# The last block's output projection by seven half products, two tile pairs in turn, with its stores in halves on two queues

## Chip, cores, metric

The kernel runs on one core of one Trainium2 chip. The metric is the device time of one execution in microseconds (us). Most executions agree within 0.3%, so a difference of a few tenths of a microsecond in one profile needs care.

## The reference, cut to what matters

```python
def reference(q, k, v, moe_w_gate, moe_w_val, moe_w_out):
    attn = attention(q, k, v)          # 8 batches x 8 heads x 576 positions x 64, causal window of 128 ... cut
    x = attn.transpose(0, 2, 1, 3).reshape(4608, 512)
    g = x @ moe_w_gate                 # 512 -> 1536
    return (g * sigmoid(g) * (x @ moe_w_val)) @ moe_w_out      # 1536 -> 512, float32 out
```

The kernel takes the 4608 tokens in nine blocks of 512. Block n (0 to 7) holds positions 0 to 511 of batch n, which are 512 neighbouring rows of the output. Block 8 is the last and holds the remaining 64 positions of each of the eight batches, so a tile of 128 of its tokens is two pieces of 64 rows, far apart in the output.

## The kernel before

A block has gate and value products (`wide`, on TensorE), an activation (ScalarE), two elementwise operations (VectorE) that give `hT`, and the projection of `hT` with `wo`. Blocks 1 to 7 project by Strassen's scheme: the 512 tokens by 512 columns are a 2 x 2 of blocks, and seven products stand in for eight. It runs on two pairs of token tiles, t = 0 and 1, each giving tile t (`top`) and tile t + 2 (`low`). The sums of `hT` that it needs are made on VectorE.

```python
def rows_of(n, j):
    if n == 8:
        return [(0, 64, 2 * j * S + 512), (64, 128, (2 * j + 1) * S + 512)]
    return [(0, 128, n * S + j * P)]

def last_project(n, j):                                  # tile 3 of the last block; tiles 0 to 2 by project()
    osb = opool.tile([P, DM], FP32, name="osb", tag="osb")
    for half in range(2):
        c = slice(half * DM // 2, (half + 1) * DM // 2)
        po = ps_a.tile([P, DM // 2], FP32, name="po", tag="a", bufs=4)
        for m in range(NMB):                             # 12 matmuls of 256 columns
            nc.tensor.matmul(po, hT[n][:, m, j * P:(j + 1) * P], wo_sb[:, m, c], ...)
        # half 0: nc.scalar.mul, half 1: nc.vector.tensor_scalar_mul, into osb[:, c]; then one store per piece of rows,
        # the first on nc.sync, the second on nc.scalar

def strassen(n, t):                                      # blocks 1 to 7
    # ... cut: views of hT and of its sums S2, S3, S4; tiles p1s, p5s, u2s, top, low
    X, Y = po[:, 0, :], po[:, 1, :]                      # the two halves of one PSUM bank
    product(X, A11, B11, True);  nc.scalar.mul(p1s, X, 0.5);  yield      # product = 6 matmuls of 256 columns
    product(p2, A12, B21, True); half_plus(top[:, 0:HC], p2, p1s);  yield
    product(X, S2, T2);          nc.scalar.mul(u2s, X, 0.5);  yield
    product(Y, S1, T1);          nc.scalar.mul(p5s, Y, 0.5);  yield
    product(X, S3, T3);          half_plus(low[:, HC:DM], X, p5s);  yield
    product(Y, S4, B22);         half_plus(top[:, HC:DM], Y, u2s);  yield
    product(X, A22, T4);         nc.scalar.mul(low[:, 0:HC], X, 0.5)
    # ... stores of top and low on nc.sync
```

The softmax here doesn't subtract the row's maximum and nothing guards it: scores larger than these inputs give would overflow.

Of the kernel before, what the change touches and what calls it, by code (L numbers as in the profile page):

```python
# [10 lines left out]
FP32 = mybir.dt.float32  # L11
# [5 lines left out]
P = 128  # L17
# [30 lines left out]
def kernel(  # L48
# [10 lines left out]
    nc = tc.nc  # L59
    B, H, S, D = q.shape  # L60
    NTOK, DM = out.shape
    DFF = moe_w_gate.shape[1]
    NKB = DM // P
    NMB = DFF // P
    NSUP = B // 2
    NBLK = NTOK // 512
# [50 lines left out]
    wo_sb = consts.tile([P, NMB, DM], FP16, name="wo_sb")  # L117
# [9 lines left out]
    supool = ctx.enter_context(tc.tile_pool(name="sup", bufs=4))  # L127
    opool = ctx.enter_context(tc.tile_pool(name="op", bufs=8))
    ps_f = ctx.enter_context(tc.tile_pool(name="ps_f", bufs=3, space=PSUM))
    ps_a = ctx.enter_context(tc.tile_pool(name="ps_a", bufs=4, space=PSUM))  # L130
# [225 lines left out]
    hT = {}  # L356
# [36 lines left out]
    def gate_val(n, m):  # L393
        c0 = 384 if (n, m) in acted else 0
        gate(n, m, wide(n, m, "g"), c0)
        yield
        val(n, m, wide(n, m, "v"), c0)
        yield

    def rows_of(n, j):  # L400
        if n == 8:
            return [(0, 64, 2 * j * S + 512), (64, 128, (2 * j + 1) * S + 512)]
        return [(0, 128, n * S + j * P)]

    def project(n, j, pool, tag, bufs):
        po = pool.tile([P, DM], FP32, name="po", tag=tag, bufs=bufs)
        for m0 in range(0, NMB, 4):
            for i in range(m0, m0 + 4):
                m = NMB - 1 - i if n == 0 else i
                nc.tensor.matmul(po, hT[n][:, m, j * P:(j + 1) * P], wo_sb[:, m, :],  # L410
                                 start=(i == 0), stop=(i == NMB - 1))
            if m0 + 4 == NMB:
                osb = opool.tile([P, DM], FP32, name="osb", tag="osb")
                nc.scalar.mul(osb, po, 0.5)
                for p0, p1, r0 in rows_of(n, j):
                    nc.sync.dma_start(out[r0:r0 + p1 - p0, :], osb[p0:p1, :])
            yield

    def last_project(n, j):

        osb = opool.tile([P, DM], FP32, name="osb", tag="osb")
        for half in range(2):
            c = slice(half * DM // 2, (half + 1) * DM // 2)
            po = ps_a.tile([P, DM // 2], FP32, name="po", tag="a", bufs=4)
            for m in range(NMB):
                nc.tensor.matmul(po, hT[n][:, m, j * P:(j + 1) * P], wo_sb[:, m, c],
                                 start=(m == 0), stop=(m == NMB - 1))
            if half == 0:
                nc.scalar.mul(osb[:, c], po, 0.5)
            else:  # L430
                nc.vector.tensor_scalar_mul(osb[:, c], po, 0.5)
            for i, (p0, p1, r0) in enumerate(rows_of(n, j)):
                (nc.sync if i == 0 else nc.scalar).dma_start(out[r0:r0 + p1 - p0, c], osb[p0:p1, c])
            yield 1.5



# [2 lines left out]
    HC = DM // 2  # L440
# [4 lines left out]
    def weight_sums(c):  # L445

        if c == 0:
            one_more.append(supool.tile([P, 1], FP32, name="one", tag="pin", bufs=1))
            nc.vector.memset(one_more[0], 1.0)
        k = slice(2 * c, 2 * c + 2)  # L450
        for t_, a, b in ((T1, B12, B11), (T3, B22, B12)):
            nc.vector.scalar_tensor_tensor(out=t_[:, k, :], in0=a[:, k, :], scalar=one_more[0],
                                           in1=b[:, k, :], op0=ALU.mult, op1=ALU.subtract)
        nc.vector.tensor_sub(T2[:, k, :], B22[:, k, :], T1[:, k, :])
        nc.vector.tensor_sub(T4[:, k, :], B21[:, k, :], T2[:, k, :])
# [4 lines left out]
    def sums(n, c):  # L460

        if n not in hsum:
            hsum[n] = [spool.tile([P, HM, 256], FP16, name=f"S{i}", tag=f"S{i}") for i in (2, 3, 4)]
        lo, hi = slice(2 * c, 2 * c + 2), slice(HM + 2 * c, HM + 2 * c + 2)
        a11, a12 = hT[n][:, lo, 0:256], hT[n][:, hi, 0:256]
        a21, a22 = hT[n][:, lo, 256:512], hT[n][:, hi, 256:512]
        s2, s3, s4 = (t_[:, lo, :] for t_ in hsum[n])
        nc.vector.tensor_sub(s3, a11, a21)
        nc.vector.tensor_add(a21, a21, a22)
        nc.vector.tensor_sub(s2, a21, a11)  # L470
        nc.vector.tensor_sub(s4, a12, s2)

    def strassen(n, t):

        h = hT[n]
        A11, A12 = h[:, 0:HM, 0:256], h[:, HM:NMB, 0:256]
        S1, A22 = h[:, 0:HM, 256:512], h[:, HM:NMB, 256:512]
        S2, S3, S4 = hsum[n]
        cols = slice(t * P, (t + 1) * P)
        po = ps_f.tile([P, 2, HC], FP32, name="po", tag="po", bufs=1)  # L480
        p2 = ps_a.tile([P, HC], FP32, name="p2", tag="a")
        top, low = (opool.tile([P, DM], FP32, name="osb", tag="osb") for _ in range(2))
        p1s = supool.tile([P, HC], FP32, name="p1s", tag="p1s", bufs=1)
        p5s = supool.tile([P, HC], FP32, name="p5s", tag="p5s", bufs=1)
        u2s = supool.tile([P, HC], FP32, name="u2s", tag="u2s", bufs=1)

        def product(dst, a, b, start=False):
            for m in range(HM):
                nc.tensor.matmul(dst, a[:, m, cols], b[:, m, :], start=(start and m == 0),  # L489
                                 stop=(m == HM - 1), skip_group_check=True)  # L490

        def half_plus(dst, a, b):
            nc.vector.scalar_tensor_tensor(out=dst, in0=a, scalar=0.5, in1=b,
                                           op0=ALU.mult, op1=ALU.add)

        X, Y = po[:, 0, :], po[:, 1, :]
        product(X, A11, B11, True)
        nc.scalar.mul(p1s, X, 0.5)
        yield
        product(p2, A12, B21, True)  # L500
        half_plus(top[:, 0:HC], p2, p1s)
        yield
        product(X, S2, T2)
        nc.scalar.mul(u2s, X, 0.5)
        yield
        product(Y, S1, T1)
        nc.scalar.mul(p5s, Y, 0.5)  # L507
        yield
        product(X, S3, T3)
        half_plus(low[:, HC:DM], X, p5s)  # L510
        yield
        product(Y, S4, B22)
        half_plus(top[:, HC:DM], Y, u2s)
        yield
        product(X, A22, T4)
        nc.scalar.mul(low[:, 0:HC], X, 0.5)
        for j, osb in ((t, top), (t + 2, low)):
            for p0, p1, r0 in rows_of(n, j):
                nc.sync.dma_start(out[r0:r0 + p1 - p0, :], osb[p0:p1, :])
        yield  # L520



    AT = {2, 3, *range(5, 10), *range(11, 18)}
# [1 line left out]
    def ffn():  # L526

        for n in range(NBLK):
            if n > 1:
                parts = chain(strassen(n - 1, 0), strassen(n - 1, 1))  # L530
            if n == 1:
                for j in range(PRE):
                    for _ in project(0, j, ps_f, "po", 1):
                        yield 1.0
            for m in range(NMB):
                for half, _ in enumerate(gate_val(n, m)):
                    yield 1.0
                    if n > 1 and 2 * m + half in AT:
                        next(parts)
                        yield 0.75  # L540
                if n == 1:
                    if m % 2 and PRE + m // 2 < 4:
                        for _ in project(0, PRE + m // 2, ps_f, "po", 1):
                            yield 1.0
                    if m in (2, 4, 6):
                        weight_sums(m // 2 - 1)
                if 0 < n < NBLK - 1 and m >= 9:
                    sums(n, m - 9)
            if n > 1:
                assert next(parts, None) is None  # L550
        for j in range(3):
            for _ in project(NBLK - 1, j, ps_a, "a", 4):
                yield 1.0
        yield from last_project(NBLK - 1, 3)


    loaded = done_t = 0
# [187 lines left out]
```

## Time and profile before

| | before |
|---|---|
| time, median (range) | 356.23 us (356.14 to 356.53), 3 runs |
| last gate or value product ends | 340.15 |
| last matmul ends | 350.56 |
| last store is issued (evacuation ended 351.00) | 351.03 |
| last packet of the last store | 352.88 |
| span ends | 354.46 |

The ends of the last value product, of the last matmul and of the last evacuation are read from the chain of waits; issue and packet times are the trace's instruction and packet records. Three views of the kernel before follow. First, of the page: busy time by engine, and the transfers that bring instructions (packets, MB, share).

```profile
span 354.5 us, 7261 instructions
...
PE 341.5 (96%) x2765; PEld 197.5 (56%) x2765; DVE 273.4 (77%) x599; ACT 178.9 (50%) x355; POOL 106.9 (30%) x132
...
q8 instruction: 21, 0.34, 0.4%
```

The q8 line counts 21 blocks of 16 KB of instructions. Second, the DMA view of the last stores, from 349.4 to 353.4 us, in fortieths of 0.1 us (GB/s):

```profile
GB/s 0 0 0 225 246 184 246 123 205 185 205 246 205 184 266 62 195 205 184 215 369 175 10 0 0 0 0 72 195 184 174 328 215 113 31 0 0 0 0 0
```

From 351.7 to 352.1 nothing moves: the last store has the DMA engines to itself. Third, the issues of the last two stores, each in two halves (duration in ns: shortest, median, longest; then when):

```profile
L433 ACTq DMA_DIRECT2D out_dram<-osb x2: 498/540/583, 349.7 to 351.0; - x2
...
L433 SPq DMA_DIRECT2D out_dram<-osb x2: 467/506/544, 349.8 to 351.0; - x2
```

An issue of 64 rows holds its queue for about half a microsecond.

### The profile page before, as it was taken

The page shows a single profiled execution, that of the slowest core. Times are in us where ns is not written, and L with a number is a line of the kernel's source. Part 1 is how long each engine was busy: PE and PEld are TensorE (multiplying, and loading weights), DVE is VectorE, ACT ScalarE, POOL GpSimd, SP SyncE. Part 2 cuts the span into 40 slices and gives each one's busy share as a digit, 9 for nine tenths or more (in the row PEclk, how much of TensorE's full clock was granted, in tenths as well). Part 3 has the DMA queues.
Part 4 walks back from the last instruction along what each step waited for, and adds up shares of the span by engine and source line. Part 5 has one row for each costly group of instructions (what it writes and reads, how often), then busy time and mean ns, then how long its engine had stood idle before and what let it go on. Part 6 is the DMA issues. An engine that isn't in the chain of part 4 may idle for free.

```text
span 354.5 us, 7261 instructions
## 1 busy us (share of the span) xinstructions
PE 341.5 (96%) x2765; PEld 197.5 (56%) x2765; DVE 273.4 (77%) x599; ACT 178.9 (50%) x355; POOL 106.9 (30%) x132
## 2 busy tenths in 40 slices
PE   7889999999999999999999999999999999999995
PEld 4684555444456655565456555664665566556643
DVE  4867976997987799678986998799878965975540
ACT  6845584555555455665556455455444323332321
POOL 8966655544848445544300100000000000000000
PEclk9999999999999999999999999999999999999999
DMA  9999999999999999999995513311022101101114
GB/s 152 170 186 187 141 176 155 99 147 137 157 142 196 146 158 163 157 167 153 165 62 105 83 39 32 88 33 58 17 75 61 44 2 59 62 0 62 41 42 96
DMA packets 157763, 37.34 MB, mean 105 GB/s; under 512 B 147232, under 2 KB 153248, under 8 KB 157728
## 3 DMA queue, kind: packets, MB, share of 16 engines
q0 software_dynamic: 116224, 18.62, 79.8%
q1 hardware_dynamic: 41056, 17.97, 27.6%
q8 instruction: 21, 0.34, 0.4%
q10 hardware_dynamic: 448, 0.30, 0.3%
q14 instruction: 14, 0.11, 0.1%
HBM read 37.91 MB, written 9.44 MB: 134 GB/s over the span
## 4 chain that ended last, share of the span: by engine, by line
PE 73%; DVE 16%; ACT 7%; issue 3%; DVEq 0%; ACTq 0%
PE pv L369 20%; PE pg L369 20%; PE po L489 14%; PE av L320 4%; DVE uu L384 4%; DVE hT L391 3%; PE ps L255 3%; PE po L410 3%; DVE ex L264 3%; PE p L489 2%; ACT ex L260 2%; PE px L346 2%; ACT tt L383 2%; ACT exc L287 2%; DVE x L323 1%
## 5 line engine op out<-in xcount | busy, mean ns | idle before, releaser
L369 PE MATMUL pg<-xT,wg_sb 128*128 128x512 f16 (+2 forms) x464 | 116.0, 365 | 0.6 <-DVE uu L384 0.3
L369 PE MATMUL pv<-xT,wv_sb 128*128 128x512 f16 (+2 forms) x464 | 114.5, 364 | 0.8 <-DVE uu L384 0.4
L383 ACT ACTIVATE tt<-pg 128x512 f16<-128x512 f32 (+2 forms) x110 | 65.5, 596 | 85.2 <-PE pg L369 81.8
L384 DVE SCALAR_TENSOR_TENSOR uu<-tt,pg 128x512 f16<-128x512 f16 (+2 forms) x109 | 73.4, 674 | 34.6 <-ACT tt L383 33.9
L391 DVE TENSOR_TENSOR hT<-uu,pv 128x512 f16<-128x512 f16 (+2 forms) x110 | 74.0, 673 | 7.1 <-PE pv L369 2.2
L369 PEld LDWEIGHTS <-wv_sb 128*128 128x128 f16 x464 | 42.8, 98 | 37.4 <-issue 3.3
L369 PEld LDWEIGHTS <-wg_sb 128*128 128x128 f16 x464 | 42.5, 98 | 36.1 <-issue 3.5
L260 ACT ACTIVATE ex<-ps 128x512 f16<-128x512 f32 x96 | 50.2, 605 | 10.1 <-PE ps L255 10.1
L169 POOL DMA_DIRECT2D va<-in_v_dram x40 | 34.1, 856 | 53.0 <-PE av L320 36.9
L175 POOL DMA_DIRECT2D qn<-in_q_dram x39 | 33.6, 864 | 24.4 <-DMA qT<-qn 14.8
L175 POOL DMA_DIRECT2D kn<-in_k_dram x39 | 33.2, 859 | 25.7 <-DMA kT<-kn 18.4
L264 DVE TENSOR_TENSOR ex<-ex,m_reg 128x1024 f16<-128x1024 f16 x48 | 32.6, 687 | 10.3 <-ACT ex L260 10.3
L489 PEld LDWEIGHTS <-hT 128*128 128x128 f16 x336 | 31.8, 98 | 15.5 <-issue 3.6
L489 PEld LDWEIGHTS <-S 128*128 128x128 f16 x252 | 23.9, 98 | 11.8 <-issue 2.9
L323 DVE TENSOR_TENSOR x<-av,rec 128x256 f16<-128x256 f32 x72 | 29.0, 420 | 0.6
L489 PE MATMUL po<-T,hT 128*128 128x256 f16 x168 | 23.1, 272 | 0.5
L489 PE MATMUL po<-T,S 128*128 128x256 f16 x168 | 23.0, 273 | 0.6 <-ACT p5s L507 0.6
L287 ACT ACTIVATE exc<-psc 128x512 f16<-128x512 f32 x40 | 21.4, 608 | 3.4 <-PE psc L283 3.4
L347 ACT COPY xT<-px 128x512 f16<-128x512 f16 x24 | 14.1, 586 | 14.9 <-PE px L346 14.8
L320 PEld LDWEIGHTS <-ex 128*128 128x128 f16 x384 | 18.4, 97 | 4.9 <-issue 0.7
L320 PE MATMUL av<-va,ex 128*128 128x65 f16 x384 | 20.4, 193 | 0.5
L410 PE MATMUL po<-wo_sb,hT 128*128 128x512 f16 x84 | 19.7, 379 | 0.0
(74 smaller groups left out, 291.0 us busy)
## 6 DMA issues: line engine op xcount, KB each, us to landing
out_dram<-osb SPq DMA_DIRECT2D x32, 256.0 KB, 2.8
va<-in_v_dram POOLq DMA_DIRECT2D x32, 128.0 KB, 7.5
qn<-in_q_dram POOLq DMA_DIRECT2D x31, 128.0 KB, 8.2
kn<-in_k_dram POOLq DMA_DIRECT2D x31, 128.0 KB, 8.1
wo_sb<-in_moe_w_out_dram POOLq DMA_DIRECT2D x2, 768.0 KB, 9.3
wg_sb<-in_moe_w_gate_dram POOLq DMA_DIRECT2D x2, 512.0 KB, 10.5
wv_sb<-in_moe_w_val_dram POOLq DMA_DIRECT2D x2, 512.0 KB, 11.8
out_dram<-osb SPq DMA_DIRECT2D x6, 128.0 KB, 2.4
```

The source lines that it names most:

```text
L169: nc.gpsimd.dma_start(va[rank][p0:p1, :, 0:D], src)
L175: nc.gpsimd.dma_start(t_[p0:p1], src)
L260: nc.scalar.activation(e[:, o:o + 2, :], banks[q4][par], AF.Exp, scale=scale)
L264: nc.vector.tensor_mul(e[:, o, :], e[:, o, :], reg[:, o, :])
L320: nc.tensor.matmul(av[:, j, :], w, val, start=(n == 0), stop=(n == len(todo) - 1))
L323: nc.vector.tensor_mul(x[:, 4 * half:4 * half + 4, :], av[:, :, 0:D], rec.broadcast_to([P, 4, D]))
L369: nc.tensor.matmul(ps[:, c0:c1], w[:, kb, ms], xT[n][:, kb, c0:c1], start=(kb == 0 and c0 == 0), stop=(kb == NKB - 1 and c1 == 512), skip_ ...
L383: nc.scalar.activation(tt, pg[:, c0:c1], AF.Tanh, scale=0.5)
L384: nc.vector.scalar_tensor_tensor(out=uu, in0=tt, scalar=one if (n, m) == PIN else 1.0, in1=pg[:, c0:c1], op0=ALU.add, op1=ALU.mult)
L391: nc.vector.tensor_mul(hT[n][:, m, c0:c1], acted[(n, m)][1][:, c0:c1], pv[:, c0:c1])
L410: nc.tensor.matmul(po, hT[n][:, m, j * P:(j + 1) * P], wo_sb[:, m, :], start=(i == 0), stop=(i == NMB - 1))
L489: nc.tensor.matmul(dst, a[:, m, cols], b[:, m, :], start=(start and m == 0), stop=(m == HM - 1), skip_group_check=True)
```

## The change

The last block, too, is projected by seven products. As no other products stand between them there, the two pairs take turns. One pair gets other buffers, the evacuations of the seventh products are on VectorE (in the earlier blocks they are on ScalarE), and all of the last block's stores go out on two queues, as only its last tile's did before: the lower 64 rows on sync and the upper 64 on ScalarE's.

```diff
+    def store(n, j, osb, c0=0, c1=512, two=False):
+        for i, (p0, p1, r0) in enumerate(rows_of(n, j)):
+            (nc.scalar if two and i else nc.sync).dma_start(out[r0:r0 + p1 - p0, c0:c1],
+                                                            osb[p0:p1, c0:c1])
-    def last_project(n, j):
...
+        end = n == NBLK - 1
+        pool, tag, bufs = (ps_a, "a", 4) if end and t else (ps_f, "po", 1)
...
         product(X, S3, T3)
         half_plus(low[:, HC:DM], X, p5s)
+        if end and t:
+            store(n, t + 2, low, HC, DM, True)
         yield
         product(Y, S4, B22)
         half_plus(top[:, HC:DM], Y, u2s)
+        store(n, t, top, 0, DM, end)
         yield
         product(X, A22, T4)
-        nc.scalar.mul(low[:, 0:HC], X, 0.5)
...
+        if end:
+            nc.vector.tensor_scalar_mul(low[:, 0:HC], X, 0.5)
+        else:
+            nc.scalar.mul(low[:, 0:HC], X, 0.5)
+        store(n, t + 2, low, 0, HC if end and t else DM, end)
         yield
...
-                if 0 < n < NBLK - 1 and m >= 9:
+                if n > 0 and m >= 9:
                     sums(n, m - 9)
...
-        for j in range(3):
-            for _ in project(NBLK - 1, j, ps_a, "a", 4):
-                yield 1.0
-        yield from last_project(NBLK - 1, 3)
+        ends = [strassen(NBLK - 1, t) for t in range(2)]
+        for t in 7 * (0, 1):
+            next(ends[t])
+            yield 0.75
```

More of the change, by code (lines that the diff above doesn't have):

```diff
@@ L414, in project @@
                 nc.scalar.mul(osb, po, 0.5)
-                for p0, p1, r0 in rows_of(n, j):
-                    nc.sync.dma_start(out[r0:r0 + p1 - p0, :], osb[p0:p1, :])
+                store(n, j, osb)
             yield
-    def last_project(n, j):
-        osb = opool.tile([P, DM], FP32, name="osb", tag="osb")
-        for half in range(2):
-            c = slice(half * DM // 2, (half + 1) * DM // 2)
-            po = ps_a.tile([P, DM // 2], FP32, name="po", tag="a", bufs=4)
-            for m in range(NMB):
-                nc.tensor.matmul(po, hT[n][:, m, j * P:(j + 1) * P], wo_sb[:, m, c],
-                                 start=(m == 0), stop=(m == NMB - 1))
-            if half == 0:
-                nc.scalar.mul(osb[:, c], po, 0.5)
-            else:
-                nc.vector.tensor_scalar_mul(osb[:, c], po, 0.5)
-            for i, (p0, p1, r0) in enumerate(rows_of(n, j)):
-                (nc.sync if i == 0 else nc.scalar).dma_start(out[r0:r0 + p1 - p0, c], osb[p0:p1, c])
-            yield 1.5
     HM = NMB // 2
@@ L479, in strassen @@
         cols = slice(t * P, (t + 1) * P)
-        po = ps_f.tile([P, 2, HC], FP32, name="po", tag="po", bufs=1)
+        end = n == NBLK - 1
+        pool, tag, bufs = (ps_a, "a", 4) if end and t else (ps_f, "po", 1)
+        po = pool.tile([P, 2, HC], FP32, name="po", tag=tag, bufs=bufs)
         p2 = ps_a.tile([P, HC], FP32, name="p2", tag="a")
         top, low = (opool.tile([P, DM], FP32, name="osb", tag="osb") for _ in range(2))
-        p1s = supool.tile([P, HC], FP32, name="p1s", tag="p1s", bufs=1)
-        p5s = supool.tile([P, HC], FP32, name="p5s", tag="p5s", bufs=1)
-        u2s = supool.tile([P, HC], FP32, name="u2s", tag="u2s", bufs=1)
+        if end and t:
+            spare = [opool.tile([P, DM], FP32, name="osb", tag="osb") for _ in range(2)]
+            p1s, p5s, u2s = spare[0][:, 0:HC], spare[0][:, HC:DM], spare[1][:, 0:HC]
+        else:
+            p1s, p5s, u2s = (supool.tile([P, HC], FP32, name=i, tag=i, bufs=1)
+                             for i in ("p1s", "p5s", "u2s"))
         def product(dst, a, b, start=False):
@@ L510, in strassen @@
         half_plus(low[:, HC:DM], X, p5s)
+        if end and t:
+            store(n, t + 2, low, HC, DM, True)
         yield
@@ L513, in strassen @@
         half_plus(top[:, HC:DM], Y, u2s)
+        store(n, t, top, 0, DM, end)
         yield
         product(X, A22, T4)
-        nc.scalar.mul(low[:, 0:HC], X, 0.5)
-        for j, osb in ((t, top), (t + 2, low)):
-            for p0, p1, r0 in rows_of(n, j):
-                nc.sync.dma_start(out[r0:r0 + p1 - p0, :], osb[p0:p1, :])
+        if end:
+            nc.vector.tensor_scalar_mul(low[:, 0:HC], X, 0.5)
+        else:
+            nc.scalar.mul(low[:, 0:HC], X, 0.5)
+        store(n, t + 2, low, 0, HC if end and t else DM, end)
         yield
```

## The prediction

> **What bounds the kernel now.** I read the page's slices first, to see which engine fills the span and where.
>
> ```profile
> PE   7889999999999999999999999999999999999995
> DVE  4867976997987799678986998799878965975540
> ACT  6845584555555455665556455455444323332321
> PEclk9999999999999999999999999999999999999999
> ```
>
> TensorE is at 90% or more in all but the first three slices and the last one, at the full clock (the view of the cores gives 1.000). So the time is TensorE's stream plus what stands before and after it. The change touches the last block only, so next I read the chain that ended last, from 336 us on (columns: start, length, what).
>
> ```profile
> 339.29 0.86 PE pv L369 x4
> 340.15 7.77 PE po L410 x36
> 347.92 2.63 PE po L426 x24
> 350.56 0.02 issue
> 350.58 0.42 DVE osb L431
> ```
>
> The gate and value products of the last block end at 340.15. The last projection is 36 matmuls of 512 columns (0.216 us each) and 24 of 256 columns (0.110 us each), one after the other without a gap: 10.40 us. From 350.56 the tail has nothing of TensorE: 0.44 us until the last evacuation ends at 351.00, then the stores, and the span ends at 354.46, that is **3.90 us** after the last matmul. The whole last projection is on the path; the earlier blocks already use seven products, but the last does not.
>
> **What the Trainium skill says.** "TensorE: Matmul & The Clock Gate", section Back-to-back issue gap, gives 262 cycles of 2.4 GHz for 256 columns and 518 for 512, which is 109 and 216 ns. The trace agrees (2.63/24 and 7.77/36), so a product costs by its columns, and halves are not dearer than wholes. "PSUM — Partial Sum Buffer", section PSUM bank collisions raise a hardware error, asks for a guard by bank, not by address. In the trace the products of a pair, whose two results X and Y share a bank, have waited for the evacuation of the other half:
>
> ```profile
> its engine sat idle before it (us, times) until:
>   issue: 6.5, 19
>   ACT p5s L507: 0.6, 2
> ```
>
> "DMA: Bandwidth & Descriptors", section Issuing engines are not separate DMA queues, says that a second queue saves issue time only, because all run on the same 16 engines; its section Rules for kernel authors adds that two transfers to disjoint partition halves serialize. The trace agrees only in part, see below.
>
> **The change part by part.**
>
> *Products.* Removed: 4 row tiles x 12 products of 512 columns, 10.40 us. Added: 2 pairs x 7 products x 6 matmuls of 256 columns = 84 x 0.1096 = 9.20 us. Saved on the path: **1.20 us**. (Of eight half products one falls away; 1/8 of 10.40 is 1.30, and the 2.5 ns or so that each of more, shorter matmuls carries takes the rest.)
>
> *Sums.* Twelve VectorE operations are added, four for each of three column groups, 0.418 us each by their rows (L468 to L471): 5.0 us on an engine that is idle most of the last 20 us. What they do to TensorE I take from block 7, where the same sums stand at the same place, and compare with block 8 (columns: start, length):
>
> ```profile
> 301.90 0.82 PE L489 MATMUL po<-wo_sb,S 128*128 128x256 f16 x6
> ...
> 308.71 1.02 PE L369 MATMUL pv<-xT,wv_sb 128*128 128x512 f16 x4
> ```
> ```profile
> 332.41 0.82 PE L489 MATMUL po<-wo_sb,S 128*128 128x256 f16 x6
> ...
> 339.13 1.03 PE L369 MATMUL pv<-xT,wv_sb 128*128 128x512 f16 x4
> ```
>
> From the pair's sixth product to the last value product block 7 takes 6.81 us and block 8, without sums, 6.72. So the sums cost 0.09 us there, and E, the end of the last value product, moves from 340.15 to 340.24.
>
> *Are the inputs there in time?* In block 7 the last hT was done 2.60 us after that product's start (311.31 less 308.71), hence at E + 1.58. The first product of each pair needs only early columns (E to E + 1.32); the second needs the last hT at its sixth matmul, at E + 1.86. That fits with 0.28 us to spare. S2 needs two more sums, in series 0.46 + 0.42, or one evacuation more: E + 2.5 to 2.9; its last third is read at E + 3.1. It fits.
>
> *Waits between products of one pair.* An evacuation starts 0.10 us after its product and takes 0.38 (ScalarE) or 0.42 (VectorE); with about 0.05 for the signal the bank is free again 0.53 or 0.57 us after. The other pair's product lies between and lasts 0.66. Hidden, with only 0.09 us to spare; this is what taking the pairs in turn buys.
>
> *The last evacuation* was on VectorE before (0.425) and is so after: nothing. On ScalarE it would be 0.384 but stand behind DMA issues of about half a microsecond there.
>
> TensorE's end: 350.56 + 0.09 - 1.20 = **349.45**.
>
> *Stores.* Here part of it is given back. Before, the outputs left in turn: 256 KB every 2.6 us, with only 128 KB in two queues at the end. After, both pairs finish together. Writing T for the end of the last matmul, the evacuations end and the stores are issued near T - 2.1 (128 KB), T - 1.45 (256), T - 0.8 (256), T - 0.1 (256), T + 0.45 (128): 1 MB in 2.6 us. The last block's stores are cut in halves of 64 rows. What such a store moves is in the DMA view of two stretches, of one store of 128 rows and of two of 64 rows on one queue (GB/s by fortieths):
>
> ```profile
> GB/s 0 0 66 262 393 393 360 426 393 393 295 492 393 230 99 0 0 0 0 0 0 0 0 229 328 295 393 393 492 295 393 393 360 393 197 33 0 0 0 0
> ```
> ```profile
> GB/s 0 0 287 164 205 287 205 164 123 328 123 164 369 41 123 246 287 205 287 164 205 246 164 205 123 287 82 123 42 0 0 0 0 0 0 0 0 0 0 0
> ```
>
> With 128 rows some 390, with 64 rows some 190 GB/s. Against the page, halves on two queues need not be slow together: in the present last store (packets 352.15 to 352.88) the packets of 1 KB take 80 ns while one queue is active and 46 ns while both are. I estimate 320 GB/s with both queues, 0.41 us for 128 KB and 0.82 for 256. A store issued now moves its first packet 1.12 us later (351.03 to 352.15). Then the stores end near T - 0.2, T + 0.75, T + 1.6, T + 2.4 and the last at T + 2.8, where before it was at T + 2.32 (352.88). So the last store, which had the engines to itself, queues for about **0.45 us**.
>
> Sum: -1.20 + 0.09 + 0.45 = -0.66; 356.23 becomes **355.6 us**.
>
> **The rivals.**
> *The stores hide.* If the transfers overlap fully, the tail is 3.90 us as before, and the time 355.1. For it: the two-queue packets at 46 ns, near 350 GB/s. Against: 1 MB has to move in about 3 us.
> *The stores become the bound.* If two queues give no more than the 190 to 200 GB/s of one, 1 MB takes 5.3 us from T - 0.95, ending at T + 4.3: a tail 2.0 us longer, and the time 357.1. For it: the page's sentence on halves, and the 64-row stores of this trace. Against: the mixed packets. A middle of 250 GB/s ends at T + 3.2, time 356.0.
> *A wait takes the place of the products.* If an evacuation misses its 0.66 us slot by 0.1 us at each of the five changes per pair, at most 1.0 us comes back, time 356.6; a late hT or S2 would cost a few tenths once. For it: margins of 0.09 and 0.28 us. Against: the evacuations have no other work beside them, and block 7 shows the sums in time.
> *The instruction order shifts.* Order outside the first stage is the scheduler's (block 7 has three sums ahead of their place). If first products of the last block were pulled ahead of the last value products, the second ones would wait for hT, up to 1.2 us. I give that little.
>
> **Range and chances.** The products' gain is firm, 1.1 us to within 0.15. The stores decide the rest: 0 to 1.2 us likely given back. So 355.6, and 354.9 to 356.5 eight times in ten; the side above is longer because of the second and third rivals. Two per cent is 7.1 us, half of the whole last projection with its tail (10.40 + 3.90), so within 2% is all but sure.
>
> **What would show it.** The chain should have 84 matmuls of L489's product at 0.66 us a group, ending near 349.5 with no evacuation between them. If the gap from E to the last matmul is over 9.4 us, the waits rival is right, and the waits view names ACT or DVE. From the last matmul to the end I expect 4.35 us against 3.90. About 3.9 says that the stores hide; 5 or more says that they bind, and the DMA view after T would be full at about 200 GB/s. The last hT should end 1.6 us after the last value product's end. The prediction is wrong outside its range if the scheduler moved things before 330 us, or if two queues do not add up.

## The result

The changed kernel takes **356.43 us** (356.22 to 356.61, 4 runs) beside 356.19 us (356.06 to 356.53, 4 runs) for the kernel before. The ratio is 1.0005, 95% interval 0.9988 to 1.0022: the same. The result is correct. The time lies inside the predicted range, at its upper edge: 0.66 us of gain were forecast and none came.

The profile after, the same lines of the page as before:

```profile
span 354.7 us, 7334 instructions
...
PE 339.8 (96%) x2789; PEld 199.0 (56%) x2789; DVE 279.9 (79%) x618; ACT 178.9 (50%) x357; POOL 106.7 (30%) x132
...
q8 instruction: 22, 0.36, 0.5%
```

TensorE works 1.7 us less, the span is not shorter, and one block of instructions more is fetched. The chain that ended last (start, length, what; L481 is `product`):

```profile
325.13 0.66 PE po L481 x6
...
339.39 0.89 PE pv L369 x4
340.28 1.31 PE po L481 x12
341.59 1.31 PE p L481 x12
342.90 6.70 PE po L481 x60
349.60 0.02 issue
349.62 0.42 DVE osb L512
```

The product on the line at 325.13 is the same one that started at 324.98 before. All TensorE instructions up to 334 us are the same in both kernels, and the offset of about 0.15 us is there from 20 us on: it is an accident of the start, not of the change. The last value product ends at 340.28 (before 340.15), so the sums cost nothing beyond that offset. The projection is now 1.31 + 1.31 + 6.70 = 9.32 us (before 10.41), and the last matmul ends at 349.60 (before 350.56). The span ends at 354.70. So the **tail** after the last matmul is 5.10 us, where it was 3.90. The DMA view of the stores, same stretch as before (GB/s; then KB each and us to landing):

```profile
GB/s 0 0 225 225 328 369 369 369 328 369 349 287 246 164 82 123 266 307 328 348 328 287 369 307 184 246 246 369 338 328 338 359 277 164 31 10 0 0 0 0
...
out_dram<-osb ACTq DMA_DIRECT2D x2, 128.0 KB, 3.3
out_dram<-osb SPq DMA_DIRECT2D x2, 128.0 KB, 2.7
```

No gap is left in front of the last store, and the rate is mostly 250 to 370 GB/s. The store issues on both queues over the whole run (of the 37 on sync, 32 are of whole tiles, at about 332 ns):

```profile
L407 SPq DMA_DIRECT2D out_dram<-osb x37: 332/333/853, 86.9 to 350.6; - x37
L407 ACTq DMA_DIRECT2D out_dram<-osb x5: 562/779/847, 347.4 to 350.6; - x5
```

On ScalarE's queue an issue of 64 rows takes 0.56 to 0.85 us, the last two begin at 350.59 and 350.61, half a microsecond after their evacuation ended at 350.04, and the last packet ends at 352.96.

So the account of the spans is: start offset +0.13, projection -1.09, tail +1.20, together +0.24 us (354.46 to 354.70).

### The profile page after: what moved, and what is told of

Read it like the earlier page. It is cut to its first block, busy times and chain, and to the rows that moved or that the text cites. A ratio compares the mean times of both kernels' runs of the same rounds, so it can differ in the third digit from the quotient of the medians. Undisturbed runs are those within 1.5% of the kernel's fastest.

```text
span 354.7 us, 7334 instructions
## 1 busy us (share of the span) xinstructions
PE 339.8 (96%) x2789; PEld 199.0 (56%) x2789; DVE 279.9 (79%) x618; ACT 178.9 (50%) x357; POOL 106.7 (30%) x132
## 4 chain that ended last, share of the span: by engine, by line
PE 70%; DVE 16%; ACT 8%; issue 3%; DMA 1%; ACTq 0%; DVEq 0%
PE pv L369 21%; PE pg L369 20%; PE po L481 16%; PE av L320 4%; DVE uu L384 4%; DVE hT L391 3%; PE p L481 3%; PE ps L255 3%; ACT ex L260 3%; DVE ex L264 3%; PE px L346 2%; ACT exc L287 2%; ACT tt L383 1%; DVE x L323 1%; DMA stage<-distance 1%
## 5 line engine op out<-in xcount | busy, mean ns | idle before, releaser
L481 PEld LDWEIGHTS <-hT 128*128 128x128 f16 x384 | 36.4, 98 | 16.3 <-issue 3.5
L481 PEld LDWEIGHTS <-S 128*128 128x128 f16 x288 | 27.4, 98 | 12.3 <-issue 2.9
L481 PE MATMUL po<-T,S 128*128 128x256 f16 x192 | 26.0, 273 | 0.6 <-ACT p5s L499 0.6
L481 PE MATMUL po<-T,hT 128*128 128x256 f16 x192 | 26.1, 272 | 0.5
L255 PE MATMUL ps<-qT,kT 64*128 64x256 f16 x192 | 17.3, 272 | 1.1 <-DVE qT L207 0.8
```

Of the source, the lines that this page charges most:

```text
L481: nc.tensor.matmul(dst, a[:, m, cols], b[:, m, :], start=(start and m == 0), stop=(m == HM - 1), skip_group_check=True)
```

## The experiments

All runs in one table. T is the end of the last matmul; the next three columns count from T. The time is the median, the ratio is to the kernel before in the same rounds. T is of a single profile and carries the accidents of its start; the columns counted from T do not. Issue and data times are from the instruction and packet records.

| run | what it changes in the changed kernel | T | last issue | last data | tail | time | ratio |
|---|---|---|---|---|---|---|---|
| (before) | | 350.56 | +0.47 | +2.32 | 3.90 | 356.19 | |
| (changed) | | 349.60 | +1.01 | +3.36 | 5.10 | 356.43 | 1.0005 |
| half_bytes | half the bytes, badly chosen | 350.93 | +0.47 | +2.19 | 3.77 | 356.30 | 0.9998 |
| one_issue | one transfer of 128 rows per store (wrong rows) | 349.34 | +0.47 | +2.69 | 4.09 | 355.26 | 0.9971 |
| in_series | seven products alone, pairs in series | 356.91 | +0.94 | +2.96 | 4.59 | 363.08 | 1.0190 |
| as_ready | each half stored when ready | 349.38 | +1.45 | +3.12 | 4.80 | 356.17 | 0.9997 |
| fetch_early | instruction fetch out of the way | 349.43 | +0.69 | +3.20 | 5.07 | 356.46 | 1.0027 |
| mid_half | half the bytes, order kept | 349.32 | +0.69 | +2.42 | 4.10 | 355.33 | 0.9976 |
| best | as_ready, fetch early, X and Y in two banks | 349.57 | +0.99 | +2.65 | 4.29 | 355.71 | 0.9990 |
| act_last | last evacuations on ScalarE | 349.46 | +1.06 | +3.27 | 4.98 | 356.24 | 1.0003 |
| swap | blocks 7 and 8 in the other order | 349.31 | +0.47 | +2.21 | 3.78 | 355.00 | 0.9967 |
| swap_ready_banks | swap, as_ready, two banks | 349.44 | +0.47 | +1.82 | 3.21 | 354.26 | 0.9946 |
| one_queue | all stores on the sync queue | 349.05 | +3.80 | +5.48 | 7.04 | 358.11 | 1.0056 |
| mid_rows | half stores from partitions 32 to 95 | 349.54 | +0.80 | +2.86 | 4.50 | 355.87 | 0.9990 |

(Tails in the expectations are some hundredths off these, since I had measured them between slightly different points.) Theories at the start: the tail grew because ten issues of 64 rows hold two queues longer than the evacuations leave them (**issue**), or because 1 MB in 2.6 us is more than such stores can move (**bandwidth**).

### half_bytes: half the bytes, and a confounded run

```diff
+        if n == NBLK - 1:
+            c1 = (c0 + c1) // 2
```

> The changed kernel with every store of the last block moving only the first half of its columns: the same ten store issues, half the bytes (0.5 MB). Wrong result on purpose. T is the end of the last matmul; the tail T to end of span was 3.90 us before and 5.05 us changed, where the last two issues started 0.99 us after T and the last data landed 2.36 us after that. Theory 'issue' (each pair of 64-row issues occupies both issuing queues for 0.6 to 0.95 us, and the evacuations come every 0.66): the last issue stays late, at T + 0.8 or more, and only the 0.5 us of transfer backlog goes: tail 4.4 to 4.6, time 0.5 to 0.6 us below the changed kernel. Theory 'bandwidth' (the issues are late because the engines are full): the last issue moves to T + 0.5 and the tail to 3.9, time 1.1 us below.

The time did not fall, but not for the reason that I tested. The left half of `top` depends on the second product only, so the scheduler let its store go then. On ScalarE's queue that store stood ahead of an evacuation. The chain shows it (start, length, what; L409 is the store, L498 an evacuation, L483 the products):

```profile
344.11 0.79 ACTq L409
...
344.94 0.39 ACT u2s L498
...
345.38 5.55 PE po L483 x48
```

TensorE waited and T moved to 350.93, 1.3 us later. The run says nothing on the two theories, except that stores that come 0.66 us apart with little to move leave a tail of 3.77. It also shows what a store on a computing engine's queue can do.

### one_issue: one transfer for each store

```diff
+        if n == NBLK - 1:
+            r0 = rows_of(n, j)[0][2]
+            nc.sync.dma_start(out[r0:r0 + P, c0:c1], osb[:, c0:c1])
+            return
```

> The changed kernel with each store of the last block as ONE transfer of 128 rows on the sync queue (to wrong rows on purpose, since the right ones lie in two ranges): five issues instead of ten, the same 1 MB. Theory 'issue': five issues of about 0.33 us are on time (last at T + 0.5), tail 3.6 to 4.0, time 1.0 to 1.4 us below the changed kernel. Theory 'bandwidth': 1 MB in 2.6 us still queues, tail 4.4 or more.

The tail is 4.09 us and the time 1.05 us below the kernel before (0.9971, interval 0.9958 to 0.9985). The last issue was on time. Nearly all data had moved by T + 2.1; the last 18 packets ended up to 0.6 us later. This stays compatible with both theories: 128 rows need half the issues and also move at some 380 GB/s.

### in_series: the seven products alone

```diff
-        end = n == NBLK - 1
+        end = False
...
-        ends = [strassen(NBLK - 1, t) for t in range(2)]
-        for t in 7 * (0, 1):
-            next(ends[t])
-            yield 0.75
+        for _ in chain(strassen(NBLK - 1, 0), strassen(NBLK - 1, 1)):
+            yield 0.75
```

> The seven products alone, in the form that the earlier blocks have: pair 0 wholly before pair 1, X and Y in one bank, last evacuation on ScalarE, all stores on the sync queue. My theory of the waits: with no other pair's product between, four changes per pair wait 0.53 to 0.57 us and the second pair's first product waits once: the last matmul some 4.5 to 5 us later than in the changed kernel, the tail about 4.4 (512 KB at the end), time 4 us above the changed kernel. Rival (the scheduler or the queue hides them): within 1 us of it.

The rival falls, and my figure was too small: T is 7.3 us later, not 4.5 to 5. The timeline of the second pair (start, length, instruction, and in brackets the wait before it and for whom):

```profile
350.67 0.81 PE L481 MATMUL po<-T,S 128*128 128x256 f16 x6 [0.53 <-ACT p1s L490]
...
352.01 0.81 PE L481 MATMUL po<-T,hT 128*128 128x256 f16 x6 [0.53 <-ACT u2s L496]
...
353.36 0.81 PE L481 MATMUL po<-T,S 128*128 128x256 f16 x6 [0.53 <-ACT p5s L499]
...
354.75 0.81 PE L481 MATMUL po<-wo_sb,S 128*128 128x256 f16 x6 [0.57 <-DVE osb L485]
```

A product starts every 1.35 us where the stream gives one every 0.66: each waits for an evacuation, ten times some 0.69 us (I had counted nine). The view states the wait as 0.53 because it counts from the modelled end of the last matmul. A group of six that keeps the stream going for 0.66 us takes 0.81 to end. **The 0.16 us of drain belong to the wait and I had left them out.** It is this that spoils the margin in the changed kernel, see below. Taking the pairs in turn is what makes the seven products possible here: in the earlier blocks' form they cost 1.9%.

### as_ready: store each half when it is ready

```diff
         half_plus(top[:, 0:HC], p2, p1s)
+        if end:
+            store(n, t, top, 0, HC)
...
-        store(n, t, top, 0, DM, end)
+        store(n, t, top, HC if end else 0, DM, end)
         (and low in two halves for both pairs)
```

> The changed kernel, but each 128 x 256 half of the last block's outputs is stored as soon as it is evacuated: the top left halves leave after the second product (sync queue alone, in time that is free), so that from the fifth product on every 0.66 us brings one store of 128 KB, two issues of some 0.57 us on two queues. Right result. Theory 'issue': the last issue at T + 0.5, the tail 3.9 to 4.1, time 1.0 us below the changed kernel, 0.8 to 1.0 below the kernel before. Rival: if halves of 64 rows cost as much in any form, the tail stays at 5.

A miss: 0.9997, tail 4.80. The reason is in the issues. One on ScalarE's queue took 1.60 us and one on the sync queue 0.95, at 347.2 to 348.8, and after them the issues of 0.55 us plus their gaps follow each other every 0.65 us: as slowly as the evacuations come, so that the delay is never made up. The last began at T + 1.45. In the packet records a block of TensorE's instructions (16 KB, on one DMA engine, 0.93 us) moves at 347.47, in the middle of this. In the changed kernel such a block moves at 347.62 for 0.95 us; in the kernel before none came near the end. That made a third theory, **fetch**.

### fetch_early: the instruction block out of the way

```diff
-        for _ in range(n):
-            nc.tensor.matmul(t_, idle[:, 0:P], idle, start=True, stop=True)
+        for _ in range(4 * n):
+            nc.tensor.matmul(t_[:, 0:P], idle[:, 0:P], idle[:, 0:P], start=True, stop=True)
         (and the two idle matmuls before the first q, in the same way)
```

> The changed kernel with its idle matmuls of the first 6 us each cut in four of 128 columns: the same columns, 54 more TensorE instructions before everything else, and nothing changed in the order after that. New theory 'fetch': TensorE's instructions arrive in blocks of 16 KB by a transfer that holds one DMA engine for about 0.95 us; the changed kernel has 48 TensorE instructions more than before, so one more block is fetched, and it fell at 347.6, in the middle of the last stores. With 54 instructions more in front, the same fetch comes some 3 us earlier (about 344.7), ahead of the first of these stores. Theory 'fetch' expects the tail after the last matmul to fall from 5.05 to 4.0 to 4.4 us and the time by 0.6 to 1.0. Theories 'issue' and 'bandwidth' expect the tail at 4.8 to 5.1 still.

The block moved to 343.64, ahead of the stores, as meant, and the last issue came earlier (T + 0.69 instead of 1.01). The tail stayed at 5.07. The DMA view from 348.9 to 352.9 us shows why (GB/s; then the sync queue, ScalarE's queue and an instruction queue: packets, MB, share):

```profile
GB/s 225 215 205 246 143 205 123 287 226 328 410 328 431 389 410 267 266 307 225 307 246 287 287 184 246 328 246 307 307 297 328 359 318 216 72 31 21 0 0 0
...
q1 hardware_dynamic: 321, 0.46, 42.5%
q10 hardware_dynamic: 371, 0.49, 39.1%
q14 instruction: 1, 0.01, 0.5%
```

The engines are busy without any pause until 352.2, often at only 200 to 300 GB/s; an earlier issue just waits longer. The fetch theory falls for the changed kernel. Whether a fetch holds up issues that meet it is not shown: in best an issue took 1.90 us beside a block at 343.98, but in half_bytes and act_last issues that began while a block moved took 0.47 to 0.58 us, no more than elsewhere. (The median, 356.46 us, has two of six runs at 358, with a granted clock of 0.993 and 0.995; the 357.19 us of best, whose start was changed in the same way, has 0.994, and the other runs of both have 0.997 to 1.0. The cause was not looked for.)

### mid_half: half the bytes, order kept

```diff
+            c = slice(c0 + (c1 - c0) // 4, c1 - (c1 - c0) // 4) if n == NBLK - 1 else slice(c0, c1)
-            ... out[r0:r0 + p1 - p0, c0:c1], osb[p0:p1, c0:c1]
+            ... out[r0:r0 + p1 - p0, c], osb[p0:p1, c]
```

> half_bytes done properly: each store of the last block moves the middle half of its columns, so that it needs the same evacuations as before and the instruction order stays that of the changed kernel (the first try let the top stores go early on the ScalarE queue and held up the evacuations there). Ten issues, half the bytes; the instruction fetch stays where it is, at about 347.6. Wrong result on purpose. 'Bandwidth' expects the last issue at T + 0.5 and the tail at 3.8 to 4.0. 'Fetch' expects the issues after 348 to be late again, tail 4.4 to 4.8. 'Issue' expects the last issue at T + 0.8 or more and the tail at 4.4 to 4.6.

The instructions of TensorE and VectorE stood in the order of the changed kernel, and the trace shows the first store on ScalarE's queue only at 347.13, after all of ScalarE's evacuations. The tail is 4.10 us, with ten issues as before and the last still late, at T + 0.69. So bytes are what most of it is: **1.0 of the 1.20 us goes with half of them**. What is left over the kernel before, 0.2 us, is as much as the last issue is later (0.69 against 0.47); that it comes from there is inferred. The DMA view from 349.1 to 353.1 us (GB/s) ends at T + 2.4. Its rate is only some 190 GB/s: with half the columns the packets are half as large too, so the run changes more than the bytes.

```profile
GB/s 184 174 236 225 164 185 225 225 154 215 225 195 31 41 164 205 174 277 205 143 149 185 93 82 169 77 5 0 0 0 0 0 0 0 0 0 0 0 0 0
```

### best: as_ready with the fetch early, and X and Y in two banks

```diff
+        if end:
+            Y = (ps_f if t else ps_a).tile([P, HC], FP32, name="py", tag="gv" if t else "a")
...
-        product(Y, S1, T1)
+        product(Y, S1, T1, end)
```

> fetch_early, plus each half column block stored as soon as it is ready (as_ready), plus X and Y of a pair in banks of their own, so that no product waits for the evacuation of the other half. Right result. The waits at the fifth to seventh products (0.04, 0.08 and 0.02 us) should go: last matmul 0.13 us earlier. If 'fetch' holds, the tail is 3.9 to 4.2 us and the time 0.9 to 1.3 us below the kernel before. If 'issue' holds, the tail stays near 4.9 as in as_ready.

The part about the banks came true: from the last value product to T it takes 0.14 us less than in the changed kernel and the runs that keep its order of products and one bank for X and Y. The stores did less than hoped, tail 4.29, last issue at T + 0.99 after the 1.90 us issue. 0.9990, interval 0.9975 to 1.0004: not clear of noise.

### act_last: the last evacuations on ScalarE

```diff
-            nc.vector.tensor_scalar_mul(low[:, 0:HC], X, 0.5)
+            nc.scalar.mul(low[:, 0:HC], X, 0.5)
```

> The changed kernel with the last evacuations (the seventh products') on ScalarE instead of VectorE: undoes one part of the change alone. They take 0.384 instead of 0.425 us, but now stand in ScalarE's queue behind store issues of 0.5 to 0.85 us each: I expect the last evacuation 0.3 to 0.8 us later and the time 0.3 to 0.8 us above the changed kernel. Rival: the stores are late anyway, so nothing changes (within 0.15 us).

The rival was right. The last evacuation ended 0.27 us later, behind an issue, and the time did not change (356.24 us, 1.0003), since the stores are late anyway. This part of the change is worth nothing by itself.

### swap: whole tiles at the end

```diff
+    SEQ = [0, 1, 2, 3, 4, 5, 6, 8, 7]
-        for n in range(NBLK):
-            if n > 1:
-                parts = chain(strassen(n - 1, 0), strassen(n - 1, 1))
+        for at, n in enumerate(SEQ):
+            if at > 1:
+                parts = chain(strassen(SEQ[at - 1], 0), strassen(SEQ[at - 1], 1))
...
-    ready = [4, 8, 13, 17, 22, 26, 31, 35, 36]
+    ready = [4, 8, 13, 17, 22, 26, 31, 36, 36]
```

> The changed kernel with the last two blocks of tokens taken in the other order, so that the last stores are of whole tiles of 128 neighbouring rows: one transfer each, five issues instead of ten, the same 1 MB, right result. It is one_issue with the rows right. Bandwidth theory (64-row halves move at about 195 GB/s on one queue and some 250 on two, 128 rows at 380): last data at T + 2.3 to 2.7 instead of 3.2 to 3.4, tail 3.9 to 4.2, time 0.8 to 1.2 us below the kernel before. If the early need of the last attention unit costs something (the end of the last value product later than about 340.1), that comes off.

As expected, and the result is right: 355.00 us, 0.9967 (0.9955 to 0.9980), tail 3.78. The DMA view from 348.6 to 352.6 us (GB/s; then KB and us to landing):

```profile
GB/s 92 10 0 143 389 348 389 389 389 348 389 369 389 410 389 348 430 349 369 410 389 348 430 369 277 348 348 307 113 0 0 0 0 0 0 0 0 0 0 0
...
out_dram<-osb SPq DMA_DIRECT2D x2, 256.0 KB, 2.3
```

The stores, which landed 2.7 to 3.3 us after their issue in the changed kernel, now land after 2.1 to 2.3 us and move mostly at 350 to 430 GB/s. The last one, issued at T + 0.47, still waits a little: its packets begin 1.22 us after its issue, those of the first store 0.84 us. (A block of instructions moved at 347.19 here too; the one issue that began beside it took 0.58 us where the others took 0.33 to 0.37.)

### swap_ready_banks: everything that helped, together

The edits of swap, as_ready and best's banks; nothing of the start.

> swap, with each half column block stored as soon as it is evacuated (eight stores of 128 KB, one issue of 0.33 us each) and X and Y in banks of their own. The waits at the fifth to seventh products go (last matmul 0.14 us earlier, as in best), the last issue is on time at T + 0.5, the last data at T + 2.1 to 2.3, tail 3.7 to 3.9: 1.1 to 1.4 us below the kernel before.

**354.26 us (354.10 to 354.44), 0.9946 (0.9934 to 0.9959)**, correct: it beats both kernels. The chain from the third product on:

```profile
342.88 1.31 PE po L481 x12
344.19 1.31 PE py L481 x12
345.50 1.31 PE po L481 x12
346.81 1.31 PE py L481 x12
348.12 1.32 PE po L481 x12
349.44 0.02 issue
349.47 0.42 DVE osb L516
```

Each turn of both pairs takes 1.31 us, with no wait. The last store is of 128 rows by 256 columns, issued in 0.33 us, and its data are out 1.82 us after T, where the kernel before took 2.32. The tail of 3.21 us is below what I expected, by half a microsecond.

### one_queue: two queues undone

```diff
-            (nc.scalar if two and i else nc.sync).dma_start(
+            nc.sync.dma_start(
```

> The changed kernel with all stores on the sync queue: undoes the two queues alone; instruction order on TensorE and VectorE the same. Ten issues of some 0.55 us in a row take 5.5 us from T - 2.1, so the last issue is at T + 2.6 to 3.0, at 195 GB/s the last data at T + 4.3 to 4.6, tail 6.1 to 6.4, time 1.0 to 1.4 us above the changed kernel. If two queues gave nothing (the page's sentence on halves taken strictly) it would be within 0.2 us.

The two queues are worth more than expected: without them the tail is 7.04 us and the time 1.7 us above the changed kernel (1.0056 to 1.0005 of the same kernel before). The DMA view, from 349 to 355 us in fortieths of 0.15 us (GB/s):

```profile
GB/s 75 0 150 232 205 218 150 260 191 164 164 69 96 259 218 150 178 273 177 177 178 232 205 218 205 191 246 191 205 144 225 137 28 27 157 205 48 0 0 0
```

About 190 GB/s throughout: one queue's 64-row stores, packets of 2 KB at some 160 ns. My figures put the last issue some 0.8 to 1.2 us too early: an issue takes some 0.60 us with its gap rather than 0.55, and between 349.3 and 349.8 none was issued though an evacuation had long ended; what held it up I did not find out.

### mid_rows: which rows, not how many

```diff
+            rows = slice(32, 96) if n == NBLK - 1 else slice(p0, p1)
-            ... osb[p0:p1, c0:c1]
+            ... osb[rows, c0:c1]
```

> The changed kernel, but every half store of the last block takes its 64 rows from partitions 32 to 95 of the tile instead of 0 to 63 or 64 to 127: the same ten issues, queues, bytes and order (wrong result on purpose). The Trainium skill's page on SBUF says that partitions 0 to 63 reach 8 of the 16 ports and 64 to 127 the other 8, so 32 to 95 reach all 16. If the half number of ports is what slows a 64-row store (2 KB packets of 160 ns instead of 85), the packets take some 85 ns throughout, the last data come at T + 2.4 to 2.7 instead of 3.2 to 3.4, the tail is 4.1 to 4.4 and the time 0.7 to 1.0 us below the changed kernel. If it is the small number of rows in a store, or the issue, nothing changes: tail 5.0 to 5.1.

The Trainium skill's "SBUF — State Buffer", section Door 1: The DMA port swizzle, says that the rate depends on how many of 16 ports the partitions reach, and that plus 64 switches to the other port of a cluster; partitions 0 to 63 then reach 8 of them, 32 to 95 all 16. The run agrees: packets of 2 KB take 87 ns throughout instead of up to 165. The DMA view from 349 to 353 us (GB/s):

```profile
GB/s 277 72 61 328 369 348 349 389 389 451 328 369 369 390 328 430 287 144 123 287 348 369 369 410 369 318 318 287 256 318 103 21 21 21 0 0 0 0 0 0
```

The tail is 4.50, 0.6 us below the changed kernel, about half of what the change had lost, and the time 355.87 us (356.43 for the changed kernel; the kernel before stood at 356.17 and 356.19 in the two). It was less than my 0.7 to 1.0: a lull from 350.6 to 350.9 and a last issue at T + 0.80 are left, which I put down to the ten issues. The rows go to the same places in the output as in the changed kernel, so it is not these places that slow the packets.

## Why the prediction was right or wrong

| term | predicted | measured |
|---|---|---|
| products | -1.20 | -1.23 (340.26 to 349.44 where nothing waits, 9.18; before 10.41) |
| sums on VectorE | +0.09 | 0 beyond the start offset |
| waits between products | 0 | +0.14 (0.04 + 0.08 + 0.02) |
| stores | +0.45 | +1.20 |
| start | not considered | +0.13 |

**Products: right.** 84 matmuls at 0.109 us.

**Sums and inputs: right.** The last hT and S2 were there in time. The timeline of the changed kernel, where the last line starts the two third products, whose first two thirds do not need the last sums:

```profile
341.17 0.69 DVE L391 TENSOR_TENSOR hT<-uu,pv 128x512 f16<-128x512 f16 x1
...
342.35 0.42 DVE L457 TENSOR_TENSOR S<-hT 128x512 f16<-128x512 f16 x1
...
342.74 1.47 PE L481 MATMUL po<-T,S 128*128 128x256 f16 x12
```

hT ended 1.58 us after the value product's end, as predicted, S2 at 342.77; its last third is read from about 343.2 on. The forecast of 0.09 us for the sums was itself smaller than the offset between two profiles.

**Waits hidden with 0.09 us to spare: wrong by a little.** The step was "with about 0.05 for the signal the bank is free again 0.53 or 0.57 us after". The 0.10 us to the evacuation's start had been read from the chain, where a product ends with its drain, and set against a slot of 0.66 that runs from start to start. With the drain of 0.16 the bank is free after about 0.70 (ScalarE) or 0.68 to 0.74 us (VectorE). The changed kernel shows the differences: in front of the fifth, sixth and seventh products the matmuls start 0.149, 0.189 and 0.133 us after the one before instead of 0.109. in_series shows the whole 0.69, and two banks take the 0.14 us away.

**Stores: the mechanism was right, the size was not.** This is the step that failed: "I estimate 320 GB/s with both queues", with stores "issued near T - 2.1 ... T + 0.45". First the rate. With the block of instructions out of the way (fetch_early) the last four stores, 896 KB, took 3.6 us, about 250 GB/s. The 46 ns packets from which I took 320 came from a stretch in which both queues happened to be active; here one queue was often alone, and then its packets slowed: in the changed kernel the 22 packets of 2 KB that ran while the other queue moved nothing took 158 ns (median), the other 362 took 84 ns. I had put the middle of 250 GB/s among the rivals, at 356.0. Second the issues. I had half a microsecond each in front of me and did not add them up: two in each 0.66 us leave no slack, beside each other they took up to 0.85, and the last was issued at T + 1.01. Third, the start: I took 1.12 us from the issue to the first packet for every store. In the packet records of all runs from 330 us on, a store of 128 rows on an idle queue moves its first packet 0.82 to 0.85 us after its issue begins, one of 64 rows 1.12 to 1.26 us, and one of 64 rows issued on ScalarE's queue beside one on sync 1.33 to 1.53 us. Fourth, the end: 1.58 us from the last packet to the end of the span became 1.74.

The sum has a slip as well. By its own figures (first packet 1.12 us after the issue, 0.41 or 0.82 us for each store, one after the other) the five stores end near T - 0.6, + 0.5, + 1.3, + 2.1 and + 2.5, so the term should have been 0.2 us instead of 0.45, and the forecast 355.3 us. That the written 0.45 lay nearer to the measured 1.20 was luck.

What the parts weigh: half the bytes take 1.0 of the 1.20 us away (mid_half), all 16 ports 0.6 (mid_rows), single transfers of 128 rows 1.0 to 1.3 (one_issue, swap). They overlap, since a late issue costs nothing while the engines are full, so the split between rate and issue within the 1.20 us stays open, and so does why one issue took 0.5 and the next 0.85 us (the two of 0.85 took 0.51 and 0.78 in fetch_early).

**The rivals.** "The stores hide" and "the stores become the bound" were the right pair to watch, and the truth lies between them, nearer the second. "The instruction order shifts" did not happen in the change; it did in an experiment, half_bytes.

## What to carry to other kernels

At the end of a kernel the work saved on the bounding engine counts only if the stores can follow: work that leaves in even pieces has its stores hidden, work that all finishes at once has them in line, so add up both the bytes and the issues of the last microseconds. Let the last stores be whole tiles of 128 partitions and neighbouring rows, and put irregular pieces earlier, where they are hidden; here that turned a change worth nothing into 0.3% (swap), and into 0.5% with each half stored when it was ready and X and Y in two banks. When a margin is a few hundredths of a microsecond, count both of its ends from the same point.

## What the Trainium skill lacked or had wrong

- "DMA: Bandwidth & Descriptors", section Rules for kernel authors, on transfers to two partition halves ("Don't bother — they serialize"): one 128-partition transfer is indeed better (about 380 against 190 GB/s, tail 3.78 against 5.10 us), but where halves are forced, issuing them on two queues does matter: 5.10 us of tail against 7.04 on one. It is not the issues alone: 2 KB packets took 84 ns (median) with the other queue at work, 164 ns in one_queue.
- The same page, section Issuing engines are not separate DMA queues, calls the issue "usually small relative to the DMA itself". Here, in the last stretch, an issue took 0.33 to 0.59 us for 128 rows and 0.47 to 0.85 us for 64 rows (as_ready and best had three longer ones, 0.95 to 1.90 us), about as long as the 0.69 us in which 128 KB move at 190 GB/s. I found no figure for a 64-row issue, or for two issues side by side, nor that fewer rows can take longer.
- "SBUF — State Buffer", section Door 1: The DMA port swizzle, was right and useful: 2 KB packets of 64 rows take up to 165 ns from partitions 0 to 63 or 64 to 127 and 87 ns from 32 to 95. The rule on halves does not point to it.
- "PSUM — Partial Sum Buffer", section PSUM bank collisions raise a hardware error, asks for a guard by bank. The waits of the fifth to seventh products fit that, since they went when X and Y had a bank each; what such a guard costs is not there: about 0.70 us from the end of a product's stream to the next use of its bank, 0.14 us in this change.
- "Runtime: NRT & Kernel Launch", section Instruction fetch mechanics, calls crossing a 16 KiB boundary "mostly hidden". For TensorE no stall by a fetch was seen in the last projection of any run. A block occupied a DMA engine for 0.88 to 1.38 us there. Store issues beside it took 1.60 us (as_ready) and 1.90 us (best), but no more than usual in half_bytes and act_last, so that the fetch was the cause in those two runs is not shown.
